# A block-causal attention with a gated MLP on one core: gate and val beside the attention by Strassen's seven products

## The chip, the core and the metric

The kernel runs on one core of a Trainium2 chip. The core has five engines with their own instruction queues: TensorE (PE: matmuls; its weight loads are shown as PEld), VectorE (DVE), ScalarE (ACT), GpSimd (POOL) and SyncE (SP, which here only issues DMAs). They share the on-chip memory SBUF; matmul results land in the eight banks of PSUM. The metric is the device time of one execution in microseconds (us). Before the change the median of three executions is 1207.72 us (1207.43 to 1209.42).

## The reference

Queries, keys and values are float32 of shape 8 batches x 8 heads x 576 x 64. Attention is block-causal with blocks of 64: a query sees the keys of its own block and of the blocks before it. The result, 4608 tokens x 512, goes through a gated MLP with 1536 hidden columns. The MLP's weights come as float64, the output is float32.

```python
scores = scale * np.matmul(q, k.transpose(0, 1, 3, 2))
scores = np.where(mask, scores, -1000000000.0)
attn = np.exp(scores - np.max(scores, axis=-1, keepdims=True))
attn = attn / (np.sum(attn, axis=-1, keepdims=True) + 1e-09)
x = np.matmul(attn, v)                    # then (batch * seq, heads * dim)
gate = 1.0 / (1.0 + np.exp(-(x @ w_gate)))
out = (gate * (x @ w_val)) @ w_out
```

## The kernel before

**Exactness.** Most large matmuls are done in fp32r, a fast float32 form. To keep precision each operand is split into a high part H (cast to fp32r) and a low part L (the rest), and a product is the sum of three matmuls: H by H, H by L, L by H. So `hidden` (L119 to L128) issues 12 matmuls for one 128-row block of hidden units: four chunks of 128 model columns, three matmuls each, 288 tokens wide (`TA`).

**First stage, 32 pairs.** A pair is two heads of one batch; four pairs make a batch. `prep` (K and Q transposed, scaled and split, a pair ahead), `attend` (scores, softmax, transposes of the weights, AV) and the loads are laid out by hand-written orders `FIRST` (pairs 0 to 6), `TURN` (pair 7) and `REST` (pairs 8 to 31). Pairs up to 7 (`N_FIRST`) use plain float32 scores, later ones split ones. The AV of a pair runs inside the next pair; its last step is the multiplication with the reciprocal row sums `rb` (L486, from PSUM into `xT`). `finish` (L491 to L496) then casts the high part on ACT (L493), stores `xT` to DRAM (L494) and subtracts the low part on POOL (L496).

**The MLP's first third beside it.** `F1 = 4` of the 12 hidden blocks are computed in the first stage. When a batch's four pairs are done, the generator `mlp1` (L556) yields its matmuls one by one, and the loop over the pairs puts them between the attention's matmuls, at 12 ticks a pair, `rate` of them a tick, at least `AHEAD` ticks behind the attention's newest matmul. Per batch that is 4 blocks x 2 token halves x (gate and val) x 12 matmuls (L126), then four or five token tiles of the out product (`out_mm`, 12 matmuls of 512 columns each, L135), stored as a partial result. `KEEP` is the number of matmuls of a batch that are left over to the next batch's pairs. `glu` makes tanh on ACT (L145), the product on DVE (L147), the high part on ACT (L152) and the low part on POOL (L153). The PSUM tiles come from a pool of two banks, `ps_m`.

**Weights.** The float64 weights are fetched as two 32-bit words and turned into float32 by integer and float operations on DVE with one square on ACT (`convert`, L106 to L118), then split. For the first stage that is 8 gate/val pieces and 4 pieces of w_out, spread over pairs 0 to 7 by `CONV_PLAN`. They stay in SBUF.

**Second stage.** The other eight hidden blocks are done in two groups `g` of four, over six token blocks `k` of 768. Gate and val use Strassen's scheme: the 2x2 split of model columns, hidden columns and tokens gives seven products instead of eight. Each weight unit (two of gate, two of val: `units`) holds seven sums of its weights, each as H and L (`wgv_tile`); x is summed in the same way (`x_load`, `x_sums`, `x_split`, L724). `product` issues 2 x 3 matmuls of 384 columns (L834), `unit` combines the products on DVE (L865 to L878), `out_block` does the out product (L892). The sums of group 0 are fetched, converted and split around the end of the attention: `early_work` in the last pair and after it, then `fetch_gv`, `sums_gv` (L625 to L672) and `split_gv` (L679) before the first block. Those of group 1 are converted during group 0 (`later`) and parked in DRAM (`wgv_d`, `wo_d`).

**Order.** Instructions are ordered on their engine by a scheduler; `behind` adds a pure order between two of them, `mark` and `last` remember the attention's newest instruction on an engine, so that conversions come behind it.

Of the kernel before, what the change touches and what calls it, by code (L numbers as in the profile page):

```python
# [22 lines left out]
KEEP = (52, 32)  # L23

CONV_PLAN = ({0: 2, 1: 1, 2: 1, 3: 1, 4: 1, 5: 1, 6: 1}, {5: 1, 6: 1, 7: 2})
# [15 lines left out]
def attn_glu_kernel(ctx: ExitStack, tc: tile.TileContext, q, k, v, w_gate, w_val, w_out, out):  # L41
# [17 lines left out]
    def gate_val_chunks(wg, wv, f):  # L59

        return [(dst[f][:, :, 0], dst[f][:, :, 1], src[:, f * P:(f + 1) * P].rearrange("(c p) n -> p c n", p=P))
                for dst, src in ((wg, w_gate), (wv, w_val))]

    def out_w(wo, f0, f, n):
        return [(wo[:, f, 0, j:j + n], wo[:, f, 1, j:j + n], w_out[(f0 + f) * P:(f0 + f + 1) * P, j:j + n])
                for j in range(0, DM, n)]
# [6 lines left out]
    def convert(pieces, tiles, last=None):  # L73

        def after(engine, ins):
            if last and engine in last:
                behind(ins.ins, last[engine])

        def fetch(i):
            src, (raw, *rest) = pieces[i][2], tiles(i)
            chunks = len(src.shape) == 3
            if chunks:
                dma = nc.sync.dma_start(out=raw.rearrange("p (c n) w -> p c (n w)", n=P), in_=src.bitcast(U32))
            else:
                dma = nc.sync.dma_start(out=raw, in_=src.bitcast(U32).rearrange("p (n w) -> p n w", w=2))
            after("SP", dma)
            return chunks, raw, *rest

        nxt = fetch(0)
        yield
        for i, (dH, dL, src) in enumerate(pieces):
            chunks, raw, T_, E_, sq = nxt
            if i + 1 < len(pieces):
                nxt = fetch(i + 1)

            def like(t):
                return t.rearrange("p (c n) -> p c n", n=P) if chunks else t

            lo, hi = raw[:, :, 0], raw[:, :, 1]
            if E_ is None:
                E_ = hi
            Tf, Ef = T_.bitcast(F32), E_.bitcast(F32)

            after("DVE", nc.vector.tensor_scalar(out=T_, in0=hi, scalar1=3, scalar2=0x3FFFFFF8,  # L106
                                                 op0=ALU.logical_shift_left, op1=ALU.bitwise_and))
            after("ACT", nc.scalar.activation(out=sq, in_=hi.bitcast(F32), func=AF.Square))
            nc.vector.scalar_tensor_tensor(out=T_, in0=hi, scalar=0xC0000000, in1=T_,
                                           op0=ALU.bitwise_and, op1=ALU.bitwise_or)  # L110
            nc.vector.scalar_tensor_tensor(out=Tf, in0=sq, scalar=TINY_HI * TINY_HI, in1=Tf,
                                           op0=ALU.is_ge, op1=ALU.mult)

            nc.vector.tensor_scalar(out=E_, in0=T_, scalar1=0xFF800000, scalar2=None, op0=ALU.bitwise_and)
            nc.vector.scalar_tensor_tensor(out=Ef, in0=lo, scalar=2.0 ** -52, in1=Ef, op0=ALU.mult, op1=ALU.mult)
            nc.vector.tensor_add(out=Tf, in0=Tf, in1=Ef)
            nc.scalar.copy(out=dH, in_=like(Tf))
            nc.vector.tensor_sub(out=dL, in0=like(Tf), in1=dH.bitcast(F32))  # L118
            yield  # L119

    def hidden(ps, w, xH, xL):
        n = 3 * NC
        i = 0
        for c in range(NC):
            for lh, rh in ((w[:, c, 0], xH[:, c]), (w[:, c, 0], xL[:, c]), (w[:, c, 1], xH[:, c])):
                mm = nc.tensor.matmul(ps, lhsT=lh, rhs=rh, start=(i == 0), stop=(i == n - 1))  # L126
                i += 1
                yield mm.ins  # L128

    def out_mm(ps, hH, hL, wo, nf, t):  # L130
        n = 3 * nf
        i = 0
        for f in range(nf):
            for lh, rh in ((hH, wo[:, f, 0]), (hL, wo[:, f, 0]), (hH, wo[:, f, 1])):
                mm = nc.tensor.matmul(ps, lhsT=lh[:, f, t * P:(t + 1) * P], rhs=rh, start=(i == 0), stop=(i == n - 1))  # L135
                i += 1
                yield mm.ins

    ahead = []

    def glu(pool, pg, pv, dst, n, lower):


        t = pool.tile([P, n], F32, name="t", bufs=2)
        nc.scalar.activation(out=t, in_=pg[:, :n], func=AF.Tanh, scale=0.5)  # L145
        h2 = pool.tile([P, n], F32, name="h2", bufs=2)
        mul = nc.vector.scalar_tensor_tensor(out=h2, in0=t, scalar=1.0, in1=pv[:, :n], op0=ALU.add, op1=ALU.mult)  # L147
        for ins in ahead:
            behind(mul.ins, ins)
        ahead.clear()  # L150
        for cols, hH, hL in dst:
            nc.scalar.copy(out=hH, in_=h2[:, cols])  # L152
            lower.tensor_sub(out=hL, in0=h2[:, cols], in1=hH.bitcast(F32))  # L153
# [7 lines left out]
    with ExitStack() as s2:  # L161
# [174 lines left out]
        def attend(p):  # L336
# [181 lines left out]

            return step

        W_out = []

# [246 lines left out]
        for p in range(n + 1):  # L771
# [4 lines left out]
            for what, places in (FIRST if p < N_FIRST else TURN if p == N_FIRST else REST):  # L776
# [16 lines left out]
                elif now:  # L793
                    now(what)
# [230 lines left out]
```

## Time and profile before

| | |
|---|---|
| median of three executions | 1207.72 us |
| the profiled execution | 1211.92 us |
| its span, first to last instruction | 1210.1 us |
| granted TensorE clock, mean | 0.993 |
| instructions | 20754 |
| moved by DMA | 152.52 MB |
| first / last L486 (end of a pair's attention) | 35.3 / 589.1 us |

The profile's page lists busy time by engine and by 40 equal slices of the span, the DMA queues, and groups of instructions by source line. Other views answer for a stretch of time, a line or a tile. "L126" is line 126 of the kernel before. A group's row reads: line, engine, operation, output<-inputs, shapes and count, then busy us and mean ns of one, then the engine's idle time before them and what ended it. A row of the timeline reads: start in us, length in us, engine, line, operation, count. Matmuls overlap in the engine's pipeline, so a matmul's own length is more than the distance to the next one's start.

### The profile page before, as it was taken

How to read it: one execution, taken by the hardware profiler on the slowest of the kernel's cores; microseconds unless marked ns; L12 is line 12 of the kernel's file. 1: busy time of each engine (PE TensorE's matmuls, PEld its weight loads, DVE VectorE, ACT ScalarE, POOL GpSimd, SP SyncE). 2: the span in 40 equal slices, each digit the busy share in tenths (PEclk: the TensorE clock that was granted, in tenths of full speed). 3: DMA queues.
4: the chain of work that ended last, by engine and by line, in shares of the span. 5: the costliest groups of instructions: out<-in, count | busy, mean ns of one | idle time of the engine just before them, and what ended most of it. 6: DMA issues, size and time to landing. Idle time of an engine off the chain costs nothing.

```text
span 1210.1 us, 20754 instructions
## 1 busy us (share of the span) xinstructions
PE 1167.7 (96%) x7421; PEld 1025.6 (85%) x7421; DVE 770.4 (64%) x1447; ACT 627.7 (52%) x1459; POOL 332.6 (27%) x411
## 2 busy tenths in 40 slices
PE   6989899999999999999999999999999999999996
PEld 3557789888888988888789889999999999998895
DVE  5678945356454545544899976866866655755743
ACT  6776857576676666666444453453454432422420
POOL 0123223133231331322101223123122153262331
PEclk8999999999999999999999999999999999999998
DMA  8664343543544443444243335235287154164153
GB/s 179 168 150 98 97 114 74 118 87 78 118 88 105 99 102 83 98 111 120 91 129 115 106 135 200 72 129 200 59 300 288 59 179 165 55 198 155 55 157 105
DMA packets 249112, 152.52 MB, mean 126 GB/s; under 512 B 189489, under 2 KB 209969, under 8 KB 248369
## 3 DMA queue, kind: packets, MB, share of 16 engines
q1 hardware_dynamic: 237952, 132.02, 39.5%
q10 hardware_dynamic: 11056, 19.17, 4.5%
q8 instruction: 58, 0.95, 0.3%
q14 instruction: 46, 0.37, 0.1%
HBM read 103.81 MB, written 47.33 MB: 125 GB/s over the span
## 4 chain that ended last, share of the span: by engine, by line
PE 73%; DVE 12%; DMA 6%; ACT 3%; POOL 2%; issue 2%; SPq 1%; POOLq 0%; DVEq 0%; ACTq 0%
PE b L834 19%; PE m L126 13%; PE bank L247 13%; PE m L892 9%; PE m L135 6%; PE bank L250 5%; PE b L892 5%; DMA pr<-part_d 3%; DVE XL L724 2%; POOL pr L907 1%; ACT P L375 1%; DMA XB<-xT_d 1%; DVE nm L372 1%; PE m L250 1%; PE bank L126 1%
## 5 line engine op out<-in xcount | busy, mean ns | idle before, releaser
L834 PE MATMUL b<-XH,w 128*128 128x384 f32 x1344 | 352.3, 337 | 5.0 <-DVE v L870 2.5
L834 PEld LDWEIGHTS b<-XH,w 128*128 128x128 f32 x1344 | 244.9, 188 | 12.4 <-DVE v L870 5.3
L834 PE MATMUL b<-XL,w 128*128 128x384 f32 x672 | 225.2, 336 | 0.0
L375 ACT ACTIVATE P<-bank,nm 128x512 f32<-128x512 f32 (+3 forms) x256 | 133.5, 538 | 69.7 <-DVE nm L372 59.0
L834 PEld LDWEIGHTS b<-XL,w 128*128 128x128 f32 x672 | 126.6, 188 | 1.3
L892 PE MATMUL m<-wo,hH 128*128 128x512 f32 x384 | 124.9, 391 | 0.0
L372 DVE TENSOR_REDUCE nm<-bank 128x2 f32<-128x1024 f32 (+3 forms) x128 | 105.0, 820 | 29.4 <-ACT P L375 26.8
L350 ACT COPY G<-bank 128x768 f32<-128x768 f32 (+3 forms) x140 | 93.2, 696 | 29.6 <-PE bank L250 26.2
L126 PE MATMUL m<-XH,wv 128*128 128x288 f32 x448 | 104.2, 304 | 1.7 <-DVE h L147 1.7
L126 PE MATMUL m<-XH,wg 128*128 128x288 f32 x448 | 104.2, 303 | 0.0
L247 PE MATMUL bank<-G,VS 128*64 128x320 f32 (+4 forms) x896 | 98.2, 361 | 0.0
L153 POOL TENSOR_TENSOR hL<-h,hH 128x288 fp32r<-128x288 f32 (+1 forms) x56 | 42.4, 757 | 199.6 <-ACT hH L152 190.7
L907 POOL TENSOR_TENSOR pr<-pr,pr 128x512 f32<-128x512 f32 x36 | 48.0, 1333 | 162.1 <-DMA pr<-part_d 139.5
L247 PEld LDWEIGHTS bank<-G,VS 128*64 128x64 f32 x896 | 55.9, 137 | 36.9 <-issue 3.5
L723 ACT CAST XH<-XB 128x1536 fp32r<-128x1536 f32 (+2 forms) x72 | 66.1, 938 | 34.6 <-DVE XB L721 25.1
L892 PEld LDWEIGHTS m<-wo,hH 128*128 128x128 f32 x384 | 71.9, 188 | 13.7
L857 ACT ACTIVATE g<-g 128x384 f32<-128x384 f32 x72 | 37.4, 524 | 81.6 <-DVE g L870 61.1
L724 DVE TENSOR_TENSOR XL<-XB,XH 128x1536 fp32r<-128x1536 f32 (+2 forms) x72 | 77.8, 1089 | 0.9 <-ACT XH L723 0.4
L126 PEld LDWEIGHTS m<-XH,wv 128*128 128x128 f32 x448 | 74.7, 188 | 4.0 <-DVE h L147 1.9
L392 DVE MEMSET bank<- 64x128 f32 x64 | 10.6, 165 | 105.8 <-PE bank L247 105.2
L126 PEld LDWEIGHTS m<-XH,wg 128*128 128x128 f32 x448 | 74.9, 188 | 3.2 <-issue 1.8
L250 PE MATMUL bank<-ident,P 128*128 128x128 f32 x560 | 75.4, 273 | 0.8 <-DVE rT L419 0.7
(179 smaller groups left out, 2488.4 us busy)
## 6 DMA issues: line engine op xcount, KB each, us to landing
pr<-part_d SPq DMA_DIRECT2D x72, 256.0 KB
xT_d<-xT ACTq DMA_DIRECT2D x32, 288.0 KB
XB<-xT_d SPq DMA_DIRECT2D x16, 576.0 KB
part_d<-ost SPq DMA_DIRECT2D x36, 256.0 KB
out_dram<-ost SPq DMA_DIRECT2D x36, 256.0 KB
VS<-in_v_dram SPq DMA_DIRECT2D x64, 128.0 KB
part_d<-ost ACTq DMA_DIRECT2D x32, 256.0 KB
rqk<-in_k_dram SPq DMA_DIRECT2D x108, 72.0 KB
```

The source lines that it names most:

```text
L126: mm = nc.tensor.matmul(ps, lhsT=lh, rhs=rh, start=(i == 0), stop=(i == n - 1))
L135: mm = nc.tensor.matmul(ps, lhsT=lh[:, f, t * P:(t + 1) * P], rhs=rh, start=(i == 0), stop=(i == n - 1))
L247: pe_last[:] = [nc.tensor.matmul(*args, **kw).ins]
L250: pe_last[:] = [nc.tensor.transpose(*args).ins]
L350: mark("ACT", nc.scalar.copy(out=dst, in_=src))
L372: mark("DVE", nc.vector.tensor_reduce(out=nm[:, c0:c0 + 2], in_=ps[:, :, c:c + n], axis=AX.X, op=ALU.max, negate=True))
L375: mark("ACT", nc.scalar.activation(out=Pi[:, h], in_=ps[:, h, c:c + n], func=AF.Exp, bias=nm[:, c0 + h:c0 + h + 1], accum_out=sm[:, 5 * h ...
L723: nc.scalar.copy(out=XO[j][0][:, a:b], in_=x)
L724: sub = nc.vector.tensor_sub(out=XO[j][1][:, a:b], in0=x, in1=XO[j][0][:, a:b].bitcast(F32))
L834: mm = nc.tensor.matmul(ps, lhsT=lh, rhs=rh, start=(first and k == 0), stop=(k == n - 1), skip_group_check=not first)
L892: mm = nc.tensor.matmul(po[t], lhsT=lh[:, f, t * P:(t + 1) * P], rhs=rh, start=(half == 0 and i == 0), stop=(half == 1 and i == 5))
L907: nc.gpsimd.tensor_add(out=pr[0], in0=pr[0], in1=pr[1])
```

## The change

Gate and val of the first stage use Strassen's seven products too, with sums of 7 x 128 columns for each of four weight units. All four units of the first stage no longer fit, so a ring of three tiles (`wring`) is kept; the sums are written to DRAM once (`wgv_d[0]`) and streamed back for each batch by ACT's DMA queue, four DMAs a unit (`load_w`). x of a batch is kept raw in one buffer (`RX`), summed in `finish` on POOL or DVE, and split into `X1` all at once when the fourth pair of the batch is done (`split_x`). The matmuls are dealt in groups of six, a whole product at a time. `xT` is gone; `VSs` has two buffers instead of three, `rb` one instead of two.

Six of the twelve pieces of the first stage are converted on DVE in pairs 0 to 5 (`conv`); the other six by `convert_aside`, four operations on DVE and the rest on POOL (`conv_second`, pairs 1 to 7). The weights of the second stage's group 0 are converted by `convert_aside` too, beside pairs 8 to 31, and parked in DRAM (`conv_ahead`, `wgv_d[1]`, `wo_d[1]`); at the end of the attention they are only loaded.

The diff, cut to its core:

```diff
-KEEP = (52, 32)
+KEEP = (48, 44)
+AHEAD_FROM = 8
+AH = 1
+AHEAD_TICKS = (1, 9)
+AHEAD_OPS = 2
+GROUP = 6
-CONV_PLAN = ({0: 2, 1: 1, 2: 1, 3: 1, 4: 1, 5: 1, 6: 1}, {5: 1, 6: 1, 7: 2})
+CONV_PLAN = {0: 1, 1: 1, 2: 1, 3: 1, 4: 1, 5: 1}
...
             def finish():
-                XH, XL = x_tiles(b)
-                nc.scalar.copy(out=XH[:, hp], in_=xT)
-                nc.scalar.dma_start(
-                    out=xT_d[b, hp * P:(hp + 1) * P, :], in_=xT)
-                nc.gpsimd.tensor_sub(out=XL[:, hp], in0=xT, in1=XH[:, hp].bitcast(F32))
+                nc.scalar.dma_start(out=xT_d[b, hp * P:(hp + 1) * P, :], in_=raw_x(b)[:, hp])
+                j, x = hp % KC, quarters(b)
+                if hp < KC:
+                    T4[j] = mp.tile([P, TA], F32, name=f"xs{j}")
+                    (nc.gpsimd if b else nc.vector).tensor_sub(out=T4[j], in0=x[j][0][1], in1=x[j][0][0])
+                else:
+                    eng = nc.vector if hp == NP - 1 or b == 0 else nc.gpsimd
+                    T5[j] = mp.tile([P, TA], F32, name=f"xd{j}")
+                    eng.tensor_sub(out=T5[j], in0=x[j][1][1], in1=T4[j])
+                    eng.tensor_sub(out=x[j][0][1], in0=x[j][1][1], in1=x[j][0][1])
+                if hp == NP - 1:
+                    split_x(b)
...
+        def split_x(b):
+            while n_units[0] < 4 * b:
+                next(mlp)
...
+            for lo, hi in ((0, 4), (4, 5), (5, 6), (6, 7)):
+                for j in range(KC):
+                    if lo == 6:
+                        nc.vector.tensor_sub(out=x[:, j, 1, 0], in0=x[:, j, 1, 0], in1=T5[j])
...
+                    nc.scalar.copy(out=H, in_=src)
+                    nc.vector.tensor_sub(out=Lo, in0=src, in1=H.bitcast(F32))
...
+        def load_w(g):
...
+            for j in range(KC):
+                for e in range(2):
+                    d = nc.scalar.dma_start(out=t[:, j, e].bitcast(F32), in_=wgv_d[0][g % 4, :, j, e])
+                    if last_mm:
+                        behind(d.ins, last_mm[0])
+                    yield
...
+        def convert_aside(i, raw, Q, dst, parts):
...
+            after("DVE", nc.vector.tensor_scalar(out=Tu, in0=hi, scalar1=3, scalar2=0x3FFFFFF8,
+                                                 op0=ALU.logical_shift_left, op1=ALU.bitwise_and))
+            yield
...
+                eng.tensor_scalar(out=sq_, in0=sq_, scalar1=TINY_HI, scalar2=None, op0=ALU.is_ge)
+                yield
+                eng.tensor_scalar_mul(Lf_, lo_, 2.0 ** -52)
+                yield
+                eng.tensor_mul(out=Ef_, in0=Lf_, in1=Ef_)
...
+                yield from product1(1, A, w, True)
+                p1 = mp.tile([P, TA], F32, name="p1", bufs=2)
+                nc.scalar.copy(out=p1, in_=A)
...
+                yield from product1(6, B_, w, True)
+                nc.vector.tensor_add(out=c12, in0=B_, in1=p1)
+                next(w_next, None)
...
+                yield from product1(2, A, w, False)
+                done(q, gv, 0, A)
+                next(w_next, None)
+                yield from product1(7, B_, w, False)
...
+                nc.vector.tensor_add(out=c22, in0=B_, in1=p1)
+                C = bank()[:, :TA]
+                next(w_next, None)
+                yield from product1(5, C, w, True)
+                nc.vector.tensor_add(out=c22, in0=C, in1=c22)
+                done(q, gv, 3, c22)
+                run(w_next)
+                yield from product1(4, B_, w, False)
+                nc.vector.tensor_add(out=c21, in0=B_, in1=p1)
+                done(q, gv, 2, c21)
+                yield from product1(3, C, w, False)
+                nc.vector.tensor_add(out=c12, in0=C, in1=c12)
+                done(q, gv, 1, c12)
...
-                    while acc >= 1:
+                    while acc >= (GROUP if whole[0] else -3):
...
+                    if 1 <= p < AHEAD_FROM:
+                        second_step()
+                    elif AH and AHEAD_TICKS[0] <= tick <= AHEAD_TICKS[1]:
+                        for _ in range(AHEAD_OPS):
+                            ahead_step("work")
...
-        for n, (q, gv) in enumerate(units[1:]):
-            for j in range(KC):
-                if n:
-                    done = combine(0, q, gv, j, W[q, gv][:, j])
-                else:
-                    split_gv(early[j][1], W[q, gv][:, j])
...
+        nc.sync.dma_start(out=W[u].bitcast(F32), in_=wgv_d[1][len(units) - 1])
+        wo = wop.tile([P, 4, 2, DM], F32R, name="wo2")
+        nc.sync.dma_start(out=wo.bitcast(F32), in_=wo_d[1])
```

`convert_aside` takes for each half of a piece five POOL operations (compare, scale, two products, one addition), then for gate and val four sums of 128 columns, then the cast to the high part and the subtraction of the low one. `product1` is six matmuls (two halves of the model columns, three each) of 288 columns. After the last pair, where the attention's banks are free, a unit uses three banks (`wide`).

More of the change, by code (lines that the diff above doesn't have):

```diff
@@ L121, in hidden @@
[L121 to L128, printed above, removed]
     def out_mm(ps, hH, hL, wo, nf, t):
@@ L132, in out_mm @@
         i = 0
[L133 to L153, printed above, removed]
+        order = [(hH, f, e) for f in (0, 2, 1, 3) for e in range(2)] + [(hL, f, 0) for f in (0, 2, 1, 3)]
+        for lh, f, e in order:
+            mm = nc.tensor.matmul(ps, lhsT=lh[:, f, t * P:(t + 1) * P], rhs=wo[:, f, e], start=(i == 0), stop=(i == n - 1))
+            i += 1
+            whole[0] = i == n
+            last_mm[:] = [mm.ins]
+            yield mm.ins
     def run(gen):
```

471 lines of the change are left out of this document (308 added, 163 removed).

## The prediction

> **What bounds the kernel now.** I read the busy times and slices first, to see which engine is full where, then busy times by stage, then single instructions at the stage borders.
>
> ```profile
> PE 1167.7 (96%) x7421; PEld 1025.6 (85%) x7421; DVE 770.4 (64%) x1447; ACT 627.7 (52%) x1459; POOL 332.6 (27%) x411
> ...
> PE   6989899999999999999999999999999999999996
> ```
>
> TensorE (PE) is 90% busy or more in all but four of 40 slices. The attention's last step for a pair is the L486 multiplication; pair 7's and pair 31's stand here, and the stages are cut at them:
>
> ```profile
> 147.96 0.76 DVE L486 TENSOR_TENSOR xT<-bank,rb 128x320 f32<-128x320 f32 x2
> ...
> 588.69 0.82 DVE L486 TENSOR_TENSOR xT<-bank,rb 128x320 f32<-128x320 f32 x2 [3.19 <-PE bank L247]
> ```
>
> ```profile
> 0.00:35.00 35.00, 23.90 (x128) 14.34 (x128) 18.45 (x37) 20.82 (x58) 3.44 (x18) 0.90 0.78 179
> 35.00:80.00 45.00, 40.34 (x259) 24.18 (x259) 30.03 (x64) 34.59 (x101) 7.35 (x10) 1.00 0.69 162
> 80.00:148.00 68.00, 61.40 (x457) 47.59 (x454) 61.19 (x115) 47.84 (x128) 20.12 (x25) 1.00 0.43 101
> 148.00:589.00 441.00, 438.52 (x3409) 381.24 (x3408) 226.20 (x459) 284.50 (x752) 128.24 (x211) 1.00 0.43 100
> 589.00:642.00 53.00, 50.47 (x299) 45.49 (x299) 50.34 (x106) 22.96 (x45) 3.17 (x3) 1.00 0.36 120
> 642.00:700.00 58.00, 55.79 (x295) 52.84 (x295) 57.21 (x101) 27.34 (x49) 14.13 (x11) 0.97 0.31 101
> 700.00:1210.00 510.00, 497.29 (x2585) 459.95 (x2583) 326.96 (x569) 189.67 (x329) 156.11 (x133) 0.99 0.44 149
> ```
>
> The columns after the length are PE, weight loads, DVE, ACT and POOL busy, then clock, DMA share and GB/s. Between 148 and 589 us, 24 pairs of 18.4 us, PE is idle 2.5 us in all. DVE has 226.20/24 = 9.4 us of work a pair, ACT 11.9, POOL 5.3. So a matmul less there is time less, while the others have 9.0, 6.5 and 13.1 us a pair free. From 589 to 700 us DVE is 97% full: it makes the weights of the second stage, and PE idles 2.5 + 2.2 us. Before 148 us PE idles 11.1 + 4.7 + 6.6 us. From 700 us on the work is not changed.
>
> **Matmuls removed.** A batch's gate and val take 4 x 2 x 2 x 12 = 192 matmuls of 288 columns now, and 4 units x 7 products x 6 = 168 then: 24 fewer, 192 over eight batches. Their modelled length (about 295 ns) overlaps the next one, so the price is the cadence:
>
> ```profile
> 606.00:617.00 11.00, 11.00 (x85) 11.00 (x84) 1.00 0.37 121
> ```
>
> This is L126 alone in 11 us: 11.00/85 = 129 ns. The gain is 192 x 0.129 = 24.8 us, 21.7 of it beside the attention (0.8 us a pair, 18.4 to 17.6) and 3.1 in the last batch. The out matmuls stay as many; the larger KEEP only shifts twelve of them from one batch to the next.
>
> **Conversions taken from DVE at the border.** The sums of group 0 now come from DRAM. What DVE's queue costs PE today:
>
> ```profile
> 578.53 0.85 PE L250 MATMUL bank<-ident,P 128*128 128x128 f32 x6 [0.74 <-DVE rT L419]
> ...
> 583.20 0.40 PE L126 MATMUL m<-XH,wv 128*128 128x288 f32 x1 [1.67 <-DVE h L147]
> ```
>
> In brackets is PE's idle time and who ended it. These are 2.4 us, with the 4.7 us of the two windows 7.1. I take 6; nothing and 7.1 are the ends. What is late next is the loading of the fourth tile (1.8 MB) and the out weights (2.1 MB) into space that frees with the last out matmul; the first three units of block 0, 126 matmuls of 384 columns, lie ahead of their use.
>
> **Work added beside the attention.** The nearest rows, of DVE, ACT and POOL:
>
> ```profile
> L147 DVE SCALAR_TENSOR_TENSOR h<-t,m 128x288 f32<-128x288 f32 x56 | 25.0, 446 | 54.4 <-PE m L126 48.9 <-POOL hL L153 3.8 <-ACT t L145 1.7
> ...
> L724 DVE TENSOR_TENSOR XL<-XB,XH 128x1536 fp32r<-128x1536 f32 x24 | 42.0, 1753 | 0.0
> ...
> L724 DVE TENSOR_TENSOR XL<-XB,XH 128x384 fp32r<-128x384 f32 x24 | 13.1, 559 | 0.0
> ...
> L632 DVE SCALAR_TENSOR_TENSOR cT<-raw,cT 128x512 uint32<-128x512 uint32 x24 | 16.3, 707 | 0.0
> ...
> L625 DVE TENSOR_SCALAR cT<-raw 128x512 uint32<-128x512 uint32 x24 | 10.3, 455 | 0.6 <-DMA raw<-in_moe_w_val_dram 0.6
> ...
> L493 ACT CAST XH<-xT 128x576 fp32r<-128x576 f32 x32 | 21.6, 674 | 18.3 <-DVE xT L486 17.7
> ...
> L850 ACT COPY p<-b 128x384 f32<-128x384 f32 x48 | 22.9, 476 | 25.2 <-PE b L834 21.5 <-DVE v L878 2.6 <-issue 1.2
> ...
> L723 ACT CAST XH<-XB 128x1536 fp32r<-128x1536 f32 x24 | 34.9, 1476 | 9.2 <-PE b L834 8.1 <-PE m L135 1.0
> ...
> L494 ACTq DMA_DIRECT2D xT_d<-xT x32: 321/326/361, 36.1 to 589.6; - x32
> ...
> L496 POOL TENSOR_TENSOR XL<-xT,XH 128x576 fp32r<-128x576 f32 x32 | 48.4, 1511 | 58.0 <-ACT XH L493 56.1
> ...
> L907 POOL TENSOR_TENSOR pr<-pr,pr 128x512 f32<-128x512 f32 x36 | 48.0, 1333 | 162.1 <-DMA pr<-part_d 139.5 <-DVE g L867 19.9 <-DVE ost L908 2.4
> ```
>
> DVE, per batch: 20 additions of 288 columns from PSUM at about 0.44 us (L147) = 8.8; the subtractions of the split, per half 1152 columns at 1.35 (between the two L724 rows) and four ops of 288 at 0.46, twice, = 6.4; two T sums and two low halves, 1.8. That is 17.0, or 4.3 a pair. Half a next-weight piece a pair, three L625 and one L632, adds 1.0. DVE goes from 9.4 to 14.7 of 17.6 us, 84%.
>
> ACT, per batch: minus four L493 (2.7); plus split copies of 4.8 (1152 columns about 1.1, three of 288 about 0.43, twice), four p1 copies of about 0.4, and 16 weight-load issues of 0.326. That is +8.9, or 2.2 a pair: 14.1 of 17.6, 80%.
>
> POOL: L496 goes (1.5 a pair), sums add about 0.8. A gate/val piece is ten ops of 256 columns, four of 128 and four over 896 twice, some 4,900 columns at 1333/512 = 2.6 ns = 12.6 us, half of it a pair: 10.9 of 17.6, 62%.
>
> No engine passes PE by this count. But product and evacuation alternate on two banks, with one product of 6 x 0.129 = 0.8 us and whatever attention work lies between, where 12 matmuls lay between before. The additions queue behind DVE's reductions, PE behind the additions. Two rows show the chance. At 84-90% DVE (80 to 148 us) PE idles 6.6 of 68 us, for several reasons; at DVE 97% (589 to 642) 2.5 of 53. As a share of the 24 pairs' 422 us that is 0 to 41 us. I take 10 (0.4 us a pair), by the 51% row on one side and the 97% row (5%, 20 us) on the other.
>
> The split of a batch is a burst: it waits for the four units of the batch before, and no product of its own batch runs ahead of it. What covers it is the out matmuls that KEEP leaves:
>
> ```profile
> 641.03 0.39 PE L135 MATMUL bank<-wo,hL 128*128 128x512 f32 x1
> 641.26 0.39 PE L135 MATMUL bank<-wo,hH 128*128 128x512 f32 x1
> ```
>
> 44 of them at 0.23 us, start to start, are 10 us of PE against 6.4 of DVE, with attention work besides, so I cost the burst at nothing beyond the 10 above; without the cover it would be up to 6 us a batch, most of the 41.
>
> **Weight stream.** 29 tiles of 1.84 MB, 53 MB, come over ACT's queue.
>
> ```profile
> q10 hardware_dynamic: 11056, 19.17, 4.5%
> ```
>
> That queue moved 19.17 MB in 4.5% of the span, 54 us of all 16 engines. So 53 MB take 150 us in some 510: a DMA share of 0.43 becomes about 0.72. One tile is 5 us; a unit lasts about 14. I cost it at nothing, hidden by the unit ahead. Without that cover the first product of a unit would wait up to 5 us. Each issue on ACT waits until the unit before has left its tile (a ring of three), and the exps queue behind it; it is put behind a matmul of the next unit, so that wait should be over. SP gets the raw pieces and two stores for each; the rb broadcasts queue behind them but have most of a pair's time.
>
> **Start.** Two more rows, for the sums and low halves of a piece:
>
> ```profile
> L669 DVE TENSOR_TENSOR cT<-cT 128x128 f32<-128x128 f32 x16 | 4.8, 329 | 0.1
> ...
> L679 DVE TENSOR_TENSOR w<-cT,w 128x896 fp32r<-128x896 f32 x8 | 8.5, 1090 | 2.1 <-ACT w L678 2.1
> ```
>
> Pairs 1 to 5 now carry one DVE conversion each of two L625, four L632, four L669 and one L679, 6.1 us, where a piece without sums took two and five, 4.4; and each aside piece puts three L625 and one L632 on DVE, 2.1, about 1.7 a pair. So about 3.4 us a pair comes on top of 30.03 of 45 us in three pairs (10.0 of 15): 13.4, 89%. PE idles 4.7 us of those 45 today, 10%; I take half as much again over five pairs of 15 us, +4. Pairs 5 to 7 lose today's second row of conversions and get the products instead, which I count as even. The ends are -6 (the 6.6 us idle in 80 to 148 us gone) and +15 (3 us for each of five pairs).
>
> **Sum.** The profiled execution is 1211.9 us, span 1210.1 with 1.8 around it. 1211.9 - 24.8 - 6 + 10 + 4 = 1195.1. It stands 4.2 us above the median of 1207.7; carried over, **1191**.
>
> **Rivals.**
>
> *DVE and POOL hold one another.* Same operation, beside POOL and alone:
>
> ```profile
> 579.17 1.87 POOL L496 TENSOR_TENSOR XL<-xT,XH 128x576 fp32r<-128x576 f32 x1 [6.64 <-ACT XH L493]
> ...
> 579.78 1.80 DVE L634 SCALAR_TENSOR_TENSOR cT<-cT 128x512 f32<-128x512 f32 x1
> ...
> 594.48 0.68 DVE L634 SCALAR_TENSOR_TENSOR cT<-cT 128x512 f32<-128x512 f32 x1
> ```
>
> A DVE op whose two inputs lie in SBUF took 1.80 us under a POOL subtraction, 0.68 alone: 1.1 lost. A pair gets about ten DVE ops of that kind (key and query lows, splits, h, conversions), with POOL 62% busy. At 0.45 us each DVE has 14.7 + 4.5 = 19.2 us a pair and becomes the bound in pairs 8 to 31: 24 x (19.2 - 17.6) = 38 us in place of my 10, 1219, slower. It decides from about 4 us held a pair. Against: POOL is spread over nine ticks, and sums read from PSUM are not of that kind. The Trainium skill (GPSIMD Engine Reference, section 8, Key points) says that POOL shares its SBUF interfaces with DVE and contends with DVE instructions of two SBUF inputs or of a 2-port mode. By that rule this rival comes true wherever the two overlap; the trace agrees in the row of 1.80, and no row shows POOL at 62%.
>
> *Nothing new waits.* The slack holds as between 148 and 589 us, start unchanged: 1211.9 - 30.8 - 4.2 = 1177. For: 9 us a pair free on DVE. Against: two banks.
>
> *Every product waits for its bank.* 196 products beside pairs at 0.15 us = 29 in place of 10: 1210, no change. For: 0.8 us of cover. Against: attention work between most products.
>
> *It doesn't do what it says.* A piece is about 22 steps on POOL at 18 a pair, and its store waits for the next pair's turn, so twelve pieces fill 24 pairs exactly. What is left is drained in the last pair, 13 to 25 us of POOL ahead of the second stage: about half hidden, 1200.
>
> **How the numbers follow.** Forecast 0.42, nothing waits 0.22, DVE and POOL 0.22, banks 0.10, drain 0.04. The range reaches 7 us under the second case (start and border at their good ends) and up to the price of the DVE and POOL case, 1170 to 1219. 0.2%, 2.4 us, is about what a measurement of this kernel can tell from no change. Faster: 0.42 + 0.22 + 0.04, and 0.01 of the banks, 0.69. The same: 0.07, of the banks. Slower: 0.22 and 0.02, 0.24.
>
> **What would show it.** Pairs 8 to 31 at 17.6 to 18.0 us, PE idle under 12 us there; 1344 Strassen matmuls of 288 columns at 129 ns; no DVE conversion after the last pair, and PE idle under 1 us there; DVE near 84%. Wrong: pairs over 18.4 us, DVE over 95% with its two-SBUF rows longer; PE waits for additions at the products; a start over 155 us to pair 7's L486; matmuls waiting for W's DMA.

## The result, and the profile after

The changed kernel takes 1287.97 us (median of four executions, 1283.6 to 1290.21), against 1208.24 us for the kernel before, run beside it: a ratio of 1.0655, 95% interval 1.0625 to 1.0684. It is 6.6% slower, where 1191 us was forecast and 1219 was the end of the range. The profiled execution took 1288.0 us.

The page of the changed kernel, busy times, TensorE by slice and its clock:

```profile
PE 1183.6 (92%) x7229; PEld 1023.2 (80%) x7229; DVE 878.4 (68%) x1650; ACT 641.0 (50%) x1503; POOL 521.8 (41%) x627
...
PE   6868999898888988988998999999999999999997
...
PEclk8988999999989998989999999999999999999999
```

192 matmuls are gone (7421 to 7229), yet PE's modelled busy time has grown from 1167.7 us, and the 8s now stand in the first half, where the attention is. The attention's multiplication of pairs 7 and 31, by which the stages were cut (L407 now), in the timeline of DVE:

```profile
162.87 0.78 DVE L407 TENSOR_TENSOR XB<-bank,rb 128x320 f32<-128x320 f32 x2
...
666.30 0.81 DVE L407 TENSOR_TENSOR XB<-bank,rb 128x320 f32<-128x320 f32 x2
```

So the start grew from 148.0 to 162.9 us (+14.9), and pairs 8 to 31 from 440.7 to 503.4 us (+62.7), 21.0 us a pair for 18.4. The border up to the second stage's first matmul went from 52.8 to 53.6, and the second stage from 568.6 to 566.3. Together that is +76.1 us of span. The windows by stage have the columns of those of before (PE, weight loads, DVE, ACT, POOL, clock, DMA share, GB/s):

```profile
0.00:36.00 36.00, 25.40 (x130) 15.17 (x131) 18.35 (x38) 21.41 (x62) 12.54 (x23) 0.91 0.73 181
36.00:88.00 52.00, 38.24 (x249) 22.46 (x249) 48.23 (x94) 35.84 (x102) 36.99 (x29) 1.00 0.75 179
88.00:163.00 75.00, 67.56 (x443) 51.58 (x442) 62.08 (x127) 46.33 (x125) 38.22 (x36) 0.89 0.75 204
163.00:666.00 503.00, 447.13 (x3262) 374.83 (x3261) 359.35 (x710) 306.32 (x806) 264.42 (x387) 0.96 0.75 203
666.00:720.00 54.00, 49.66 (x273) 43.23 (x272) 30.33 (x62) 20.64 (x42) 5.61 (x9) 0.97 0.87 326
720.00:1286.00 566.00, 555.58 (x2881) 515.92 (x2879) 360.03 (x624) 210.48 (x367) 164.05 (x144) 0.99 0.42 144
```

Beside pairs 8 to 31 no engine is full: DVE 71%, ACT 61%, POOL 53%. But PE is idle 503.0 - 447.1 = 55.9 us, 2.5 before, and its clock is 0.96: 4% of 503 us, about 20 us, lost. So this stage does not lack an engine's time; it waits. Two waits can be read in the timeline, the first of them here:

```profile
541.55 0.58 SPq L158 DMA_DIRECT2D rqk<-in_k_dram  x1
...
549.25 0.33 ACTq L498 DMA_DIRECT2D W<-wgv_d  x1
549.71 0.69 ACT L296 ACTIVATE P<-bank,nm 128x512 f32<-128x512 f32 x1 [6.11 <-DMA rqk<-in_k_dram]
...
551.25 0.58 PE L169 MATMUL bank<-KH,QBH 128*128 128x288 f32 x1 [4.03 <-POOL XB L590]
```

An exp needs no load of keys. What stood was the issue of a weight load ahead of it (L498). In the trace's records the 1059 DMAs of both queues take eight semaphores in turn, 132 or 133 each, and 929 of the issues wait until the transfer that had the same semaphore last has landed. Here that was a load of keys, issued by SP 7.7 us earlier, whose last part landed at 549.24 us. The exps were behind it in ACT's queue, and PE stood 4.03 us at the score of the tail queries. (The bracket names POOL, for lack of a better event; POOL's result is not an input.) Added up over the trace's records, ACT stood 31.5 us ahead of L498 and 14.3 us ahead of L413, the store of x, beside pairs 8 to 31; the kernel before stood 1.7 us ahead of such issues. The second wait is in DVE's queue:

```profile
229.07 0.78 DVE L407 TENSOR_TENSOR XB<-bank,rb 128x320 f32<-128x320 f32 x2
234.37 0.64 DVE L554 TENSOR_SCALAR XB<-XB 128x512 uint32<-128x512 uint32 x1 [4.53 <-DMA XB<-in_moe_w_gate_dram]
234.93 0.62 DVE L560 TENSOR_SCALAR XB<-XB 128x512 uint32<-128x512 uint32 x1
235.47 0.43 DVE L717 SCALAR_TENSOR_TENSOR t<-t,m 128x288 f32<-128x288 f32 x1
...
235.97 0.61 PE L688 MATMUL m<-XH,W 128*128 128x288 f32 x1 [4.20 <-DVE t L717]
```

The first operation on a raw piece of the next weights (L554) stands until its fetch has landed; the evacuation of a product (L717) is behind it, and PE stands 4.20 us for the bank. And such a wait costs twice, as the windows around the score at 551.25 show:

```profile
547.00:551.30 4.30, 0.27 (x3) 0.08 (x1) 1.97 (x6) 1.59 (x5) 4.10 (x5) 0.79 0.88 178
551.30:553.00 1.70, 1.70 (x7) 1.70 (x8) 0.00 (x0) 1.70 (x8) 0.00 (x0) 0.50 1.05 349
553.00:556.00 3.00, 3.00 (x13) 1.90 (x13) 2.90 (x5) 2.46 (x11) 1.96 (x3) 0.50 0.55 150
```

PE's clock falls to 0.50 and stays there for some microseconds after PE is back at work.

### The profile page after: what moved, and what is told of

The parts are those of the page before. It is cut to its first block, busy times and chain, and to the rows that moved or that the text cites. A ratio compares the mean times of both kernels' runs of the same rounds, so it can differ in the third digit from the quotient of the medians.

```text
span 1286.2 us, 21056 instructions
## 1 busy us (share of the span) xinstructions
PE 1183.6 (92%) x7229; PEld 1023.2 (80%) x7229; DVE 878.4 (68%) x1650; ACT 641.0 (50%) x1503; POOL 521.8 (41%) x627
## 4 chain that ended last, share of the span: by engine, by line
PE 51%; DVE 17%; DMA 13%; POOL 6%; ACT 5%; issue 4%; SPq 2%; ACTq 0%; POOLq 0%; DVEq 0%
PE b L1039 22%; PE m L1097 9%; PE bank L169 6%; PE b L1097 5%; PE m L688 5%; DMA W<-wgv_d 3%; ACT P L296 3%; PE bank L172 2%; DVE nm L293 2%; DVE XL L923 1%; SPq L158 1%; DMA wgv_d<-XB 1%; DMA rqk<-in_k_dram 1%; DMA XB<-xT_d 1%; DMA pr<-part_d 1%
## 5 line engine op out<-in xcount | busy, mean ns | idle before, releaser
L1039 PE MATMUL b<-XH,W 128*128 128x384 f32 x1008 | 270.1, 339 | 0.4 <-DVE ost L1113 0.3
L688 PE MATMUL m<-XH,W 128*128 128x288 f32 x784 | 196.8, 320 | 15.7 <-DVE t L717 7.3
L1039 PEld LDWEIGHTS b<-XH,W 128*128 128x128 f32 x1008 | 184.4, 188 | 4.1 <-DVE ost L1113 0.6
L1039 PE MATMUL b<-XL,W 128*128 128x384 f32 x504 | 169.7, 339 | 0.0
L688 PEld LDWEIGHTS m<-XH,W 128*128 128x128 f32 x784 | 139.2, 197 | 29.6 <-DVE t L717 7.8
L688 PE MATMUL m<-XL,W 128*128 128x288 f32 x392 | 119.2, 304 | 1.3 <-DVE XL L482 1.3
L1039 PEld LDWEIGHTS b<-XL,W 128*128 128x128 f32 x504 | 94.5, 188 | 1.3
L1039 PE MATMUL b<-XH,w 128*128 128x384 f32 x336 | 93.1, 338 | 1.0 <-DVE v L1075 0.4
L570 POOL TENSOR_SCALAR XB<-XB 128x256 f32<-128x256 uint32 (+1 forms) x27 | 32.2, 1192 | 140.5 <-DMA XB<-in_moe_w_val_dram 68.1
L688 PEld LDWEIGHTS m<-XL,W 128*128 128x128 f32 x392 | 77.3, 197 | 2.7 <-DVE XL L482 2.3
```

Source lines behind the costliest of these rows:

```text
L570: eng.tensor_scalar_mul(Lf_, lo_, 2.0 ** -52)
L688: mm = nc.tensor.matmul(ps, lhsT=lh, rhs=rh, start=(first and k == 0), stop=(k == 3 * KC - 1), skip_group_check=not first)
L1039: mm = nc.tensor.matmul(ps, lhsT=lh, rhs=rh, start=(first and k == 0), stop=(k == n - 1), skip_group_check=not first)
```

## The experiments

Every run is one execution with its profile. The kernel before took between 1209.17 and 1212.95 us beside them, and the four executions of the changed kernel lie 6.6 us apart, so a difference of two times under 7 us is not read as one. The diffs below show the main edits. Where the weights of the second stage's first group are not made, it loads others of the same size (`wgv_d[0]`), those of w_out in four loads for one; in dve_only both stores read the half of the buffer that DVE writes.

**Two suspects, taken away one at a time and together.** The weight loads go to SP's queue (w_on_sp), the weights are not loaded again after the first batch (no_stream), the conversion beside pairs 8 to 31 is left out (no_ahead), and the first with the third (sp_no_ahead).

```diff
 # w_on_sp, sp_no_ahead
-                    d = nc.scalar.dma_start(out=t[:, j, e].bitcast(F32), in_=wgv_d[0][g % 4, :, j, e])
+                    d = nc.sync.dma_start(out=t[:, j, e].bitcast(F32), in_=wgv_d[0][g % 4, :, j, e])
 # no_stream
+            if 3 <= g < 4 * B:
+                W1[g] = kept[(0, 0, 1, 2)[g % 4]]
+                return
 # no_ahead, sp_no_ahead
-        convs, ahead, n_ahead = conv(), conv_ahead(), [0]
+        convs, ahead, n_ahead = conv(), iter(()), [0]
```

> The weight tiles are issued on SP's queue in place of ACT's; bytes and everything else stay. Theory A (the exps stand on ACT's queue behind issues that wait for an earlier transfer; 33.3 us of such waits in pairs 8 to 31, and PE stalls of 27 us at the KH,QBH matmul with clock drops after them): 1245 to 1260 us, pairs 8 to 31 at 19.3 to 20 us in place of 21.0, KH,QBH waits nearly gone. Theory B (VectorE and GpSimd hold one another, products wait for their bank): 1280 to 1290. Theory C (the DMA traffic itself is too much): 1280 to 1290.

> The 29 weight tiles are not loaded again: later batches multiply by the three tiles of the first batch, so the fourth unit's weights are left out. No issue on ACT and 53 MB less. Theory A: like the run with the issues on SP, 1245 to 1260. Theory C: clearly lower than that run, by 15 us or more. Theory B: 1280 to 1290.

> The conversion of the next weights beside pairs 8 to 31 is left out (the second stage's first group multiplies by other weights of the same size, loaded the same way). GpSimd falls from 11 to about 4.5 us a pair. Theory A: VectorE and GpSimd are freer but the issues on ACT still wait: 1260 to 1280. Theory B: 1235 to 1255, as the waits behind VectorE go.

> Both: issues on SP and no conversion ahead. If A and B add up, their two gains together. Theory A alone: as with SP alone, within 6 us. If all of the waits are these two, 1215 to 1230, with pairs 8 to 31 near 18.0 us.

| | conversion ahead | without it |
|---|---|---|
| weight loads on ACT | 1288.0 | 1240.7 |
| weight loads on SP | 1261.7 | 1223.4 |

No_stream took 1249.4. So the place of the loads costs 17 to 26 us, the conversion ahead 38 to 47, and the two together 64.6 of the 80. No theory held alone: w_on_sp came 1.7 us above the range of A and far under that of B and C, no_ahead came where B had it, no_stream where A had it, and sp_no_ahead where 'all of the waits are these two' had it. Windows of w_on_sp and, below, of sp_no_ahead, the start and pairs 8 to 31:

```profile
0.00:161.00 161.00, 129.58 (x812) 87.07 (x813) 126.56 (x256) 102.77 (x288) 87.06 (x87) 0.93 0.74 193
161.00:639.00 478.00, 435.87 (x3272) 366.63 (x3271) 359.81 (x713) 306.05 (x808) 265.48 (x387) 0.99 0.75 217
```

```profile
0.00:163.00 163.00, 128.82 (x816) 87.12 (x817) 125.80 (x257) 103.44 (x289) 86.63 (x88) 0.93 0.74 196
163.00:602.00 439.00, 426.61 (x3267) 363.96 (x3266) 321.74 (x663) 304.02 (x806) 111.22 (x195) 1.00 0.71 198
```

With both gone, PE is idle 12.4 us there and the clock is at 1.00; the DMA share is still 0.71. So the stream of weights as such is not too much for the DMA engines. Most of what it cost came from ACT's standing at its issue (26.3 us); beside the conversion ahead, the stream on SP still cost 12.3 us (1261.7 against 1249.4 in no_stream), and which of its waits did that was not tested. But even without both, pairs 8 to 31 take 439.2 us, 1.5 less than before.

**What of the conversion ahead?** With the loads on SP: eleven empty steps between a fetch and the first use (sp_gap); of its instructions only POOL's (pool_only) or only DVE's (dve_only), with all transfers; and, without it, the six pieces of pairs 1 to 7 that POOL converts left out too (no_second; their four DVE operations go with them).

```diff
 # sp_gap
-                yield "work"
+                for _ in range(12):
+                    yield "work"
 # pool_only: the four nc.vector operations of a piece (L554 to L563) give way to
+                for _ in range(4):
+                    yield
 # dve_only
+            if parts > 1:
+                for _ in range(18 if gv else 12):
+                    yield
+                return
 # no_second, beside the two edits of sp_no_ahead
-        second = conv_second()
+        second = iter(())
```

> Issues on SP as before, and eleven empty steps between the fetch of a raw piece and VectorE's first operation on it; all work stays. Theory G (VectorE's queue stands on that first operation until the fetch lands, 17.7 us of idle VectorE in the run with SP alone, with evacuations and the AV product behind it): 1240 to 1250 us. Theory P (GpSimd's operations hold VectorE's): 1255 to 1262, no change to the run with SP alone.

> Issues on SP; of the conversion ahead only GpSimd's operations, the fetches and the stores stay, VectorE's four operations a piece are left out (the results are not used). Without any of it this kernel took 1223, with all of it 1262. Theory P: 1245 to 1260. Theory G: 1223 to 1232.

> Issues on SP; of the conversion ahead only VectorE's four operations, the fetches and the stores stay, GpSimd's are left out (the results are not used). Theory G: 1240 to 1255, VectorE still stands on the fetches. Theory P: 1223 to 1232. If each is partly right, both kernels lie between and the two excesses over 1223 add up to about 38.

> Issues on SP, no conversion ahead, and the six pieces that GpSimd converts in pairs 1 to 7 are left out too (zeros for the out weights, the third unit's weights for the fourth). If these cause the late start, pair 7's AV comes at 148 to 153 us in place of 162.7 and the kernel takes 1208 to 1214. If the denser conversions on VectorE in pairs 1 to 5 or the products cause it, the start stays over 158 and the kernel at 1218 to 1224.

Measured: 1261.2, 1255.9, 1258.3 and 1216.0 us. Half of the instructions, whichever half, costs nearly as much as all (1261.7): their sum is not the price. Theory P has sp_gap and pool_only in its ranges, theory G neither, and dve_only is above both; no_second lies between its two ranges, in time and in its start. In dve_only DVE stands at the raw piece; in pool_only POOL stands 75.2 us at its first operation for the piece's stores, and ACT 38.7 us ahead of its stores of x (added up as above). In dve_only L554 reads:

```profile
L554 DVE TENSOR_SCALAR XB<-XB 128x512 uint32<-128x512 uint32 x15 | 6.4, 426 | 34.3 <-DMA XB<-in_moe_w_out_dram 14.5 <-DMA XB<-in_moe_w_gate_dram 8.5 <-DMA XB<-in_moe_w_val_dram 7.8
```

The gap gained nothing, of which more below. No_second gives back 6.7 of the start's 14.9 us (its pair 7 comes at 156.0 us, at 162.7 in sp_no_ahead and from 159 to 164 in the other runs). In its start PE has these two windows:

```profile
36.00:88.00 52.00, 44.27 (x264) 25.74 (x264) 41.20 (x95) 39.78 (x112) 3.86 (x3) 0.95 0.68 176
88.00:156.00 68.00, 60.45 (x416) 46.00 (x417) 49.03 (x106) 40.52 (x114) 14.69 (x23) 0.94 0.72 208
```

From 36 to 88 us DVE has 41 of 52 us, where the changed kernel had 48 (93%), and PE 44, where it had 38.

**ACT without any issue.** All DMA issues of ACT in the first stage go to SP: with all work (act_free), without the conversion ahead (act_free_no_ahead), and with its transfers alone (act_free_dma_only).

```diff
 # all three, beside the edit of w_on_sp
-                nc.scalar.dma_start(out=xT_d[b, hp * P:(hp + 1) * P, :], in_=raw_x(b)[:, hp])
+                nc.sync.dma_start(out=xT_d[b, hp * P:(hp + 1) * P, :], in_=raw_x(b)[:, hp])
-                    nc.scalar.dma_start(out=part_d[r:r + P, :], in_=ost)
+                    nc.sync.dma_start(out=part_d[r:r + P, :], in_=ost)
 # act_free_dma_only
-                for _ in convert_aside(i, raw, Q, (rawf, Qf), 2):
+                for _ in range(22 if i < 4 * KC else 16):
-                for e, x in enumerate((rawf, Qf)):
+                for e, x in enumerate((Qf, Qf)):
```

> All work of the changed kernel stays; every DMA issue that ACT has in the first stage (the weight tiles, the stores of xT_d and part_d) goes to SP's queue. Theory 'lanes': an issue waits for the transfer eight issues back to land, and ACT's exps stand behind it; with no issue left on ACT its waits of some 15 us in pairs 8 to 31 go, most of PE's waits at KH,QBH go with them: pairs 8 to 31 from 477 us (weight loads alone on SP) to 460 to 468 us, the kernel 1245 to 1252 us. Rival 'the raw pieces': the waits that are left come from the fetches and stores of the conversion ahead and what stands behind them on DVE and SP; then SP with more issues is no faster: 1258 to 1270 us.

> As act_free, and the conversion ahead beside pairs 8 to 31 is left out (fetches, DVE, POOL and stores). 'Lanes' and 'the raw pieces' both expect about the time of the run with the weights on SP and no conversion ahead, 1223 us, less at most 3 us that ACT still stood there: 1219 to 1224 us. Above 1228 us SP's queue itself would be what is late.

> As act_free, but of the conversion ahead only the fetches and the stores stay; its DVE and POOL instructions are left out. If the transfers with their waits are what the conversion ahead costs, it lies within 8 us of act_free; if the instructions are, within 8 us of act_free_no_ahead; in the middle, both.

Measured: 1264.9, 1221.1 and 1229.9 us. The first falls outside what 'lanes' expected: ACT no longer stands at an issue, but the time is that of w_on_sp. The transfers alone cost 8.8 us over no conversion ahead, though the DMA share is at its highest, 0.80. The windows of pairs 8 to 31, act_free, then act_free_no_ahead, then act_free_dma_only:

```profile
163.00:645.00 482.00, 439.25 (x3269) 369.85 (x3269) 357.10 (x712) 304.80 (x808) 264.08 (x387) 0.98 0.74 213
```

```profile
163.00:600.00 437.00, 426.56 (x3265) 363.65 (x3264) 321.29 (x664) 303.85 (x807) 111.27 (x195) 1.00 0.71 197
```

```profile
162.00:609.00 447.00, 429.87 (x3261) 364.08 (x3260) 320.95 (x662) 303.38 (x805) 111.26 (x195) 1.00 0.80 230
```

So of the 44 us between the first two the transfers are 9, a little above the 8 that were the limit for 'the instructions'. The other 35 are the instructions, or their waits.

**The work without its waits.** All transfers and all instructions stay in their places in act_free, but work on separate memory (no_waits). Then the waits are put back one kind at a time: the instructions work on the fetched piece again (fetch_waits), or the stores read what the instructions wrote (store_waits).

```diff
 # no_waits
-            T, sq = Q[:, :4], Q[:, 4:]
+            T, sq = (Q[:, :4], Q[:, 4:]) if parts == 1 else (lo.bitcast(F32), hi.bitcast(F32))
-                for _ in convert_aside(i, raw, Q, (rawf, Qf), 2):
+                Qraw = Q.bitcast(U32).rearrange("p s n -> p (s n)").rearrange("p (n w) -> p n w", w=2)
+                for _ in convert_aside(i, Qraw, Q, (Qf, Qf), 2):
-                for e, x in enumerate((rawf, Qf)):
+                still = wo1.rearrange("p f e n -> p (f e n)")[:, :c * P].rearrange("p (s n) -> p s n", n=P)
+                for e, x in enumerate((still, still)):
 # fetch_waits: of these only the last edit; store_waits: all but the last, and
+                for e, x in enumerate((Qf, Qf)):
```

> As act_free, with all transfers and all DVE and POOL instructions of the conversion ahead in their places, but without the waits between them: the instructions work in the upper half of the buffer on what lies there, the fetches land in the lower half, which nothing reads, and the stores read the weights of the output, which nothing writes any more. (The weights converted ahead are thus garbage.) Theory 'head of the queue': DVE's, POOL's and SP's queues stand on an instruction of a raw piece until its transfer lands or its converted half is there, and the attention's instructions stand behind it; without those waits the time comes near that of the transfers alone (1229.9 us): 1229 to 1240 us, pairs 8 to 31 in 447 to 457 us. Rival 'the work itself' (DVE's and POOL's time for the instructions, and their share of the port): the time stays near act_free (1264.9 us): 1256 to 1268 us. In the middle, both, in that ratio.

> As no_waits, but the instructions of the conversion ahead work on the fetched raw piece again, in its place, and so wait for the fetch, and the next fetch waits for the last of them; the stores still read weights that nothing writes, and nothing waits for them. Theory 'the fetch': DVE and GpSimd stand on the landing, and that is most of the 31 us between 1234 and 1265: 1255 to 1266 us. Theory 'the stores' (SP's queue stands at the next fetch until the stores of the piece before have landed, with the loads and stores of the attention behind it): 1233 to 1242 us. In between: both.

> As no_waits, but the stores read the half of the buffer in which the instructions work: they wait for the last of these, and the next piece's instructions wait for the stores; the fetch still lands where nothing reads. 'The fetch' expects 1234 to 1241 us, 'the stores' 1250 to 1266 us.

Measured: 1234.2, 1260.6 and 1252.9 us. The rows of L554 (its last part is DVE's idle time ahead of it, over the whole span), of no_waits, store_waits, fetch_waits and act_free:

```profile
L554 DVE TENSOR_SCALAR XB<-XB 128x512 uint32<-128x512 uint32 x15 | 7.0, 468 | 0.1
```

```profile
L554 DVE TENSOR_SCALAR XB<-XB 128x512 uint32<-128x512 uint32 x15 | 6.4, 427 | 24.3 <-DMA wgv_d<-XB 20.3 <-DMA wo_d<-XB 3.6 <-DMA XB<-in_moe_w_val_dram 0.4
```

```profile
L554 DVE TENSOR_SCALAR XB<-XB 128x512 uint32<-128x512 uint32 x15 | 6.9, 461 | 31.5 <-DMA XB<-in_moe_w_val_dram 11.0 <-DMA XB<-in_moe_w_out_dram 10.3 <-DMA XB<-in_moe_w_gate_dram 10.2
```

```profile
L554 DVE TENSOR_SCALAR XB<-XB 128x512 uint32<-128x512 uint32 x15 | 6.6, 437 | 31.0 <-DMA XB<-in_moe_w_out_dram 9.6 <-DMA XB<-in_moe_w_val_dram 7.6 <-DMA XB<-in_moe_w_gate_dram 5.8
```

All four have the same instructions and transfers beside pairs 8 to 31. Where DVE stands 0.1, 24.3, 31.5 and 31.0 us at the raw piece, the kernel takes 1234.2, 1252.9, 1260.6 and 1264.9 us. The work itself is 1234.2 - 1229.9 = 4.3 us, within what two runs differ by; its waiting is 30.7. Those are the waits of all queues together, of which DVE's row is one. POOL's wait goes too, as its first product of a piece shows (no_waits, then act_free):

```profile
L570 POOL TENSOR_SCALAR XB<-XB 128x256 f32<-128x256 uint32 x24 | 22.9, 953 | 1.5
```

```profile
L570 POOL TENSOR_SCALAR XB<-XB 128x256 f32<-128x256 uint32 x24 | 25.3, 1052 | 116.3 <-DMA XB<-in_moe_w_val_dram 55.8 <-DMA XB<-in_moe_w_gate_dram 34.8 <-DMA XB<-in_moe_w_out_dram 21.5
```

In store_waits POOL stands 1.5 us there too, so its wait is not needed for the loss of 18.7 us. Either kind of wait alone brings back most of it, and the two do not add up (26.4 and 18.7 for 30.7), as would be the case if DVE, standing for the one, lets the other pass meanwhile; that was not tested further. The window of no_waits for pairs 8 to 31 shows what that looks like when it is gone:

```profile
161.00:614.00 453.00, 432.64 (x3265) 366.72 (x3264) 355.61 (x711) 304.09 (x807) 249.40 (x387) 0.99 0.78 226
```

DVE has within 2 us the work that it had in act_free, in 28 us less.

**A cure that was none.** With sp_gap's empty steps most of DVE's wait at L554 went (7.3 us, after 18.0 in w_on_sp and 19.9 in the changed kernel), but the time did not. POOL was then the next suspect: the scheduler had put its first product of a piece (L570) right behind the fetch, where it stood 137.6 us in sp_gap. Here it is held behind the comparison (gap_held), and with ACT free of issues as well (all_held).

```diff
-                eng.tensor_scalar_mul(Lf_, lo_, 2.0 ** -52)
+                low = eng.tensor_scalar_mul(Lf_, lo_, 2.0 ** -52)
+                if parts > 1:
+                    behind(low.ins, ge.ins)
```

> As sp_gap (weights on SP, 11 empty steps after each fetch, all work kept), and GpSimd's first product of a raw piece (the low word by 2**-52), which the order of the program puts ahead of the comparison, right behind the fetch, is held behind that comparison. Theory 'head of the queue, GpSimd's too': in sp_gap DVE hardly stood on a raw piece any more (6 us), but GpSimd stood on that product until the fetch landed, with the scaling of the next pair's first 128 queries (L238) behind it; held back, that wait goes: 1236 to 1250 us. Rival 'not GpSimd': what is left of sp_gap's loss comes from elsewhere (the stores, SP's queue): 1257 to 1264 us, as sp_gap's 1261.2 us.

> As gap_held, and every DMA issue of ACT in the first stage goes to SP as in act_free. ACT then never stands behind an issue. 'Head of the queue' expects it at gap_held less what ACT still stands there (up to 15 us): 1232 to 1248 us. If SP's queue with more issues makes its own waits, it is no better than gap_held or up to 5 us worse.

Measured: 1258.3 us, where the rival had it, and 1269.8 us, above what either expected. In gap_held POOL's wait is gone and DVE's nearly so:

```profile
L570 POOL TENSOR_SCALAR XB<-XB 128x256 f32<-128x256 uint32 x24 | 24.2, 1007 | 1.7
...
L554 DVE TENSOR_SCALAR XB<-XB 128x512 uint32<-128x512 uint32 x15 | 7.4, 494 | 7.4 <-DMA XB<-in_moe_w_gate_dram 3.1 <-DMA XB<-in_moe_w_out_dram 2.2 <-DMA XB<-in_moe_w_val_dram 1.6
```

POOL's standing at that product is therefore not what was left, and DVE's at L554 is not the whole loss here. Pairs 8 to 31 still take 473.2 us, and the border 56.4 (453.0 and 52.0 in no_waits), as the last piece is now late. ACT still stands 21.9 us ahead of its stores of x, and the pieces' instructions are pressed into the later steps of a pair. Whether that is the rest was not settled. All_held does not help to settle it: DVE stands 20.2 us at L554 again there, perhaps because the fetch is behind more issues on SP.

No version that was run beats the kernel before: the best, no_second, which leaves out the conversion ahead and POOL's six pieces and thus does not do the whole work, took 1216.0 us beside 1209.7.

## Why the prediction was wrong

Of the 92.9 us between its sum, 1195.1, and the profiled 1288.0 us, pairs 8 to 31 have 71.3, the start 14.0, and the border with the second stage 7.6 (with the gain of the 192 matmuls put where they run: 18.6, 3.1 and 3.1 us).

- **What bounds the kernel** was read rightly, PE beside the attention. That the other engines had 6 to 13 us a pair free was true, too, and misled: free time in an in-order queue is of use only if nothing in that queue waits for something slow.
- **Matmuls removed.** 1344 matmuls of 288 columns are there as forecast, and 144 fewer beside pairs 8 to 31 (3409 to 3265 in act_free_no_ahead). With no conversion in the way PE's busy time fell by 438.5 - 426.6 = 12.0 us there, 83 ns each and not 129. Within a product the cadence held (132 ns from start to start, median, after 133), so the missing 6.6 us lie elsewhere; where, no experiment looked.
- **Work added.** The sizes were right. DVE has 359.35/24 = 15.0 us a pair (14.7 forecast), ACT 12.8 (14.1, of which 1.3 are issues, which the views do not count as busy), POOL 11.0 (10.9); the DMA share is 0.75 (0.72).
- **Waits beside pairs 8 to 31: the step that failed.** It took 10 us, up to 41, from how full DVE is. It cost 53.4 us of PE idle and about 20 us of clock, the weight loads' part included. Fullness was the wrong scale, as no_waits shows: at DVE 78% full it takes 4.3 us more than without the instructions, where act_free at 74% takes 35.0. What the prediction priced as 0.46 us, the first operation on a raw piece, waits for a DMA and stands up to 4.5 us at the head of DVE's queue. How the 30.7 us of waits divide between the queues of DVE, POOL and SP stays open. That an added instruction is an added wait was not counted there at all, nor that the next piece's fetch waits for the stores of the one before in the same buffer.
- **Weight stream**, at nothing. "It is put behind a matmul of the next unit, so that wait should be over" failed: the wait for the ring's tile was over, but the issue also waits for a semaphore that a load of another queue had last. On SP the same issues cost 26.3 us less (17.4 without the conversion ahead).
- **Border**, -6. The conversions left DVE (97% to 56%), but the stage took 53.6 us after 52.8, with PE idle 4.3 us, 2.2 of them one wait for a combination on DVE (L739), behind which the clock was at 0.50 for 3.4 us; with the second stage's 2.3 us the gain was 1.5, where -6 and the last batch's -3.1 were forecast.
- **Start**, +4, measured +14.9, the far end of what was given (+15). DVE at 93% was forecast as 89%; the price of that was too low. PE is idle 31.8 us in the start, 22.4 before, and the clock, at which nothing was priced, is 0.89 from 88 to 163 us, 1.00 before: in two stretches at 0.50, of 10.2 and 6.8 us, half the time was lost, about 8.5 us. The longest wait, 4.24 us for DVE's multiplication (L407), ends at 87.72 us, just ahead of the first. Leaving out the conversions on POOL in pairs 1 to 7 gave back 6.7 us; what causes the rest stays open.
- **The rivals.** 'DVE and POOL hold one another' had the right sign and not the mechanism. The Trainium skill's rule (GPSIMD Engine Reference, section 8, Key points) is there in the traces: the evacuation from two SBUF inputs, L717 `v<-g,v`, takes 447 ns alone and 657 on average beside POOL. But 4.5 us a pair were priced, and DVE's whole work is 0.3 us a pair above the forecast; no_waits has both engines' instructions and loses 4.3 us in all. Of the other rivals none happened: products do wait, but behind DVE's head of queue, and nothing was left to drain at the border.

## What to carry to other kernels

When work is moved into the slack of in-order engines, price the wait of each first instruction on fetched data, not only its time: DVE at 74% with DMA waits at the head of its queue (act_free) held PE up far more than DVE at 78% without them (no_waits). Issue DMAs from an engine that computes nothing, or count what stands behind the issue; but that queue has its own waits, and moving ACT's remaining issues to SP as well gained nothing here (1264.9 after 1261.7 us). And ask of a moved stage not "is there room?" but "who is behind it when its data is late?": take the wait alone away, with the work kept in place, and see which of the two costs.

## What the runs showed of the hardware that was not expected

PE's clock fell to 0.50 after rather short gaps, and not after every one. Here after 1.70 us, in the timeline and the windows of the changed kernel:

```profile
528.95 0.55 PE L169 MATMUL bank<-KH,QBH 128*128 128x288 f32 x1 [1.70 <-ACT P L296]
```

```profile
527.30:529.00 1.70, 0.05 (x1) 0.08 (x1) 0.45 (x1) 1.64 (x5) 0.00 (x0) 0.99 1.00 309
529.00:532.40 3.40, 3.40 (x14) 2.23 (x16) 1.09 (x2) 3.12 (x12) 0.00 (x0) 0.50 1.04 388
532.40:535.00 2.60, 2.60 (x29) 1.84 (x26) 1.84 (x5) 1.19 (x5) 0.00 (x0) 1.00 1.11 367
```

The slow stretches of this trace last 3.4, 6.8 or 10.2 us. The Trainium skill (TensorE: Matmul & The Clock Gate, Part 1) has a free-running window of 3413 ns and a half clock after at least one idle window. The lengths agree with it; the gaps are shorter than its window, down to half of it, and at 289.8 us one of 2.12 us had no such effect. Short gaps seem to add up: by the trace's records PE was idle for 1.8 to 3.4 us, gaps taken together, in the 3.41 us ahead of each of the eleven falls between 25 us and the end. The gap of 1.70 us at 527 us thus cost PE 1.7 us more, half of the 3.4 us behind it.

The second lies in how this program shares its semaphores, and was not expected either: an engine's DMA issue can stand for a transfer of another queue that it has nothing to do with, as in the rows at 549.25 us.
